# Routing attention before a tanh-shrink block: sums of the first pairs moved from TensorE products to GpSimd additions, and two masks moved behind an addition

## The chip, the cores and the metric

The kernel runs on one core of a Trainium2 chip. The metric is the time of one execution on the device in microseconds (us), the median of three runs. The engines are called as in the profile: PE (TensorE's products), PEld (its weight loads), DVE (VectorE), ACT (ScalarE), POOL (GpSimd) and SP (SyncE, which here only issues DMAs). Each engine works through its own instructions in the order in which the program gives them; engines wait for one another by semaphores.

## The reference, cut to what matters

```python
# q, k, v: (4, 8, 768, 64); centroids: (8, 16, 64)
q_assign = argmax(einsum('bhsd,hcd->bhsc', q_n, c_n))      # nearest centroid of each query
k_assign = argmax(einsum('bhsd,hcd->bhsc', k_n, c_n))      # and of each key
mask = q_assign[:, :, :, None] == k_assign[:, :, None, :]
scores = where(mask, q @ k.T / 8, -1e9)
attn = exp(scores - max(scores))
attn = attn / (sum(attn) + 1e-9)
x = (attn @ v) as (3072, 512)
h = x @ w_in                                               # 512 x 2048
out = (h - tanh(h)) @ w_out                                # 2048 x 512
```

A query attends only to keys of its own centroid. The sum over the keys divides the values' products; it is this sum whose making is changed.

## The kernel before, in words

**Pairs, halves, steps.** Two heads of a batch make a pair: 4 batches of 4 pairs, numbered n = 0 to 15 (HP = 4 pairs to a batch). The 768 queries of a pair are worked on in two halves of 384; the 768 keys are six blocks of 128, two to a step. So a half of a pair has three steps (s = 0, 1, 2), and there are 96 steps in all. Steps 0 to 11 are the first halves of pairs 0 to 3, steps 12 to 23 their second halves; then pair follows pair. Batch number 2, the third, begins at step 48 (4 * HALF, with HALF = 12).

**A step.** `begin` computes the scores of both blocks, transposed (keys on partitions), with PE (L499) into PSUM; ACT takes the exponential (L521). `select` (L531, DVE) multiplies it by a mask: is the key's code, a scalar of each partition, equal to the query's code, which lies spread over all partitions in `row`? The result is the weight `e`, 128 x 2 x 384 for a block. `value` (L556, PE) multiplies `e` with the values and accumulates over the three steps. The sum over the keys is made in one of two ways:

- `summed` pairs: `sum_up` (L571) multiplies every `e` with 32 columns of ones on PE, four products a step, accumulating in PSUM over the three steps.
- all others: GpSimd adds the six `e` of the half elementwise (L543 for the first two, L547 for each of the other four), and one pair of products with 64 columns of ones at the end, in `total` (L590), sums over the partitions.

Before, `summed` holds for the first halves of pairs 0 to 3, steps 0 to 11. In these the exponential of ACT goes to SBUF and not back to PSUM. In three of them, pairs 1 to 3 (`masked`), no mask of DVE is needed: PE adds a large negative number to the scores where codes differ, by a product of one-hot codes (`hot`, made by `one_hot`, L474 and L478 on DVE, from codes that come by a DMA; the product is L510). In pair 0 DVE masks: twelve instructions whose inputs `row` and `e` both lie in SBUF. For all later masked halves the exponential lies in PSUM, and L531 reads `row` from SBUF and `sc` from PSUM.

**What stands around it.** In the first twelve steps PE also transposes queries and keys of pairs 2 and 3 (`turn`, L355), compares them with the centroids (`similar`, L376) and transposes codes for publishing (`publish`, L432, pq); DVE makes codes of the comparison (`turn_back` L386, `route` L394 to L400, `route_on` L409), and these go through DRAM back into `hot`. `begin(following)` is called inside a step before its own `value`, so scores run one step ahead. The one_hot of pair 1 stands in DVE's order behind the masks of pair 0 and in front of the routing of pair 2. The weights of the second block arrive in pieces: `fetch` (L218) issues a DMA from GpSimd's queue, ACT prepares a piece (`rest_of`, L149 and L150), DVE finishes it (`round_piece`, L158 and L161), and then issues the next fetch on GpSimd.

**What becomes of a sum.** `total` copies it by ACT (L595). For pairs 0 and 1 it is written by DMA to DRAM, read back compactly, inverted and spread (`compact`, `invert`, `spread_out`, `scale` with L692). For pairs 2 and 3 (`soon`) it stays: `pick` (L702, PE) joins the two parts that a `summed` half leaves, `divide` (L707, L710, DVE) inverts it; GpSimd keeps tallies (L597, L711).

**Order.** The order in each step is written out by hand: a list `todo` holds small pieces of work (masks first, then transposes, publishing, routing, rounding), and a list `now` holds products of the second block (`fill`) that fit into the step. `todo` is cut into as many parts as `now` has slots, and each product calls `between()`, which does the next part. From step 24 on the products of the second block are made with seven products in place of eight (Strassen's form); product 1 of a block is copied by ACT, product 2 is added to it by DVE (L928), which frees its PSUM bank. Three banks (`ps_f`) go round. Ahead of step 48's work DVE makes the differences that the later products need (`right_factors`, L899).

Of the kernel before, what the change touches and what calls it, by code (L numbers as in the profile page):

```python
# [58 lines left out]
def kernel(  # L59
# [19 lines left out]
    HP = H // 2  # L79
# [99 lines left out]
    def fast():  # L179
# [224 lines left out]
        def route_on(n: int):  # L404
            top = tops.pop(n)
            shape = [P, 2, 2, NCH] if masked(n, 0) else [P, 2, NCH, 2]
            code = codes[n] = codep.tile(shape, F32, name="code")
            if masked(n, 0):
                nc.vector.reduce_max(  # L409
                    out=code.rearrange("p h i j -> p (i j) h"),  # L410
                    in_=top.rearrange("p (g h) c -> p g h c", h=2), axis=AX.X,
                )
                return
            nc.vector.reduce_max(out=code.rearrange("p i j h -> p (i j h)"), in_=top, axis=AX.X)

        def summed(n: int, half: int):

            return n < HP and half == 0

        def masked(n: int, half: int):  # L420


            return summed(n, half) and n > 0

        def publish(n: int):

# [56 lines left out]
        xT, scores, weights, sums, avs = {}, {}, {}, {}, {}  # L483

        def weight_tiles(n: int, half: int, s: int):
            if (n, half, s) == (0, 0, NS - 1):
                return [gp.tile([P, 2, TB], F32, name="e", tag="g") for _ in range(2)]
            t = ep.tile([P, 2, 2, TB], F32, name="e")
            return [t[:, i] for i in range(2)]

        def begin(step):
            n, half, s = step
            sc = {}
            for i in range(2):
                j = 2 * s + i
                sc[i] = ps_s.tile([P, 2, 512], F32, name="sc", tag="s")
                for h in range(2):
                    r = slice(h * D, h * D + D)
                    nc.tensor.matmul(  # L499
                        sc[i][:, h, 0:TB],  # L500
                        lhsT=turned[n, 1][r].rearrange("p a n -> p (a n)")[:, j * P : (j + 1) * P],
                        rhs=turned[n, 0][r, half], start=True, stop=not masked(n, half),
                    )
            for i in range(2):
                j = 2 * s + i
                out = sc[i][:, :, 0:TB]
                if masked(n, half):
                    for h in range(2):
                        r = slice(h * D, h * D + D)
                        nc.tensor.matmul(  # L510
                            sc[i][:, h, 0:TB],
                            lhsT=hots[n][r, 1].rearrange("p a n -> p (a n)")[:, j * P : (j + 1) * P],
                            rhs=hots[n][r, 0, half], start=False, stop=True,
                        )
                if summed(n, half):
                    if i == 0:
                        weights[n, half, s] = weight_tiles(n, half, s)
                    out = weights[n, half, s][i]
                else:
                    scores[n, half, j] = sc[i]  # L520
                nc.scalar.activation(out=out, in_=sc[i][:, :, 0:TB], func=ACT.Exp, scale=SCALE)  # L521

        def select(n: int, half: int, j: int):

            if not masked(n, half):
                if j % 2 == 0 and not summed(n, half):
                    weights[n, half, j // 2] = weight_tiles(n, half, j // 2)
                e = weights[n, half, j // 2][j % 2]
                sc = e if summed(n, half) else scores.pop((n, half, j))
                for h in range(2):  # L530
                    nc.vector.scalar_tensor_tensor(  # L531
                        out=e[:, h].rearrange("p (j n) -> p j n", n=P), in0=rows[n, half][:, h],
                        scalar=(
                            codes[n][:, h, 1, j : j + 1] if masked(n, 0) else codes[n][:, 1, j, h : h + 1]
                        ),
                        in1=sc[:, h, 0:TB].rearrange("p (j n) -> p j n", n=P),
                        op0=ALU.is_equal, op1=ALU.mult,
                    )
            if j % 2 == 1 and not summed(n, half):
                pair = weights[n, half, j // 2]  # L540
                if j == 1:
                    s = sums[n, half] = sump.tile([P, 2, TB], F32, name="sum")
                    nc.gpsimd.tensor_tensor(out=s, in0=pair[0], in1=pair[1], op=ALU.add)  # L543
                else:
                    s = sums[n, half]
                    for i in range(2):
                        nc.gpsimd.tensor_tensor(out=s, in0=s, in1=pair[i], op=ALU.add)  # L547

        def value(n: int, half: int, s: int):
            e = weights.pop((n, half, s))  # L550
            if s == 0:
                avs[n, half] = ps_a.tile([P, TB], F32, name="av", tag="a")
            for i in range(2):
                j = 2 * s + i
                for h in range(2):
                    nc.tensor.matmul(  # L556
                        avs[n, half][h * D : h * D + D], lhsT=vals[n][:, h, j], rhs=e[i][:, h],
                        start=(j == 0), stop=(j == NCH - 1),
                    )
            if summed(n, half):  # L560
                weights[n, half, s] = e

        def sum_up(n: int, half: int, s: int):
            e = weights.pop((n, half, s))
            if s == 0:
                sums[n, half] = ps_f.tile([P, TB], F32, name="den", tag="f")
            for i in range(2):
                for h in range(2):

                    r = h * D + i * D // 2  # L570
                    nc.tensor.matmul(  # L571
                        sums[n, half][r : r + D // 2], lhsT=ones[:, 0 : D // 2], rhs=e[i][:, h],
                        start=(s == 0), stop=(s == NS - 1), tile_position=(0, r),
                    )
# [311 lines left out]
        def right_factors(b: int, c: int):  # L886

            if c == 0:
                diffs[b] = (
                    late_pools["diff"].tile([P, 3, CH, TB], F32, name="diff")  # L890
                    if b else half_pools["diff"].tile([P, 3, CH, TB // 2], F32, name="diff")
                )
            d = diffs[b]
            x, y = columns(b, c), columns(b, CH + c)
            for out, u, w in (
                (d[:, 0, c], x[:, 1], x[:, 0]), (d[:, 1, c], y[:, 1], d[:, 0, c]),
                (x[:, 1], y[:, 1], x[:, 1]), (d[:, 2, c], y[:, 0], d[:, 1, c]),
            ):
                nc.vector.tensor_tensor(out=out, in0=u, in1=w, op=ALU.subtract)  # L899
# [174 lines left out]
        HALF = HP * NS  # L1074
# [122 lines left out]
        route(1)  # L1197
        route_on(1)
        begin(steps[0])
        round_piece(rounding.pop(0))  # L1200
        begin(steps[1])
        publish(1)
        select(*steps[0][:2], 0)
        spread_both(1)
        begin(steps[2])
        load(1, (2,))
        load(3)
        for n in range(2, HP):
            load(n, (2,))
        select(*steps[0][:2], 1)  # L1210
        ready[1] = {**ready.get(1, {}), 5: lambda: one_hot(1)}

# [10 lines left out]
        for at, (n, half, s) in enumerate(steps):  # L1223
# [13 lines left out]
            now = []  # L1237
# [3 lines left out]
                spent += now[-1][0]  # L1241
            stages = ready.get(at, {})

            values_first = 1 in stages and not summed(n, half)
            if values_first:
                value(n, half, s)
            if 1 in stages:
# [16 lines left out]
                    rest_of(piece)  # L1264
            if not values_first:
                value(n, half, s)
            if summed(n, half):
                if 0 in stages:
                    stages.pop(0)()
                sum_up(n, half, s)  # L1270
            if s == NS - 1:
                take(n, half)
# [30 lines left out]
            if following:  # L1303
                todo += [lambda i=i: select(*following[:2], 2 * following[2] + i) for i in range(2)]

                if half == 1 and s == NS - 1 and joined(n):
                    todo.insert(len(todo) - 1, lambda n=n: total_both(n))
# [33 lines left out]
            if "raw" in late_pools:  # L1341
                todo += [check_done, check_done, check_on, check_on]
                if p == HP - 1 and half == 1 and s == NS - 2:
                    todo += [lambda b=b, c=c: right_factors(b, c) for c in range(CH - 1)]
            slots = max(sum(it[1] for it in now), 1)
            if at == 2 * HALF:
                for c in range(CH):
                    right_factors(0, c)
# [17 lines left out]
            if at in fills and "raw" in late_pools:  # L1366
                for c in range(CH - 1 if at > 4 * HALF else 0, CH):
                    right_factors(b - 1, c)
            for it in now:
                it[2](between)  # L1370
            if not now:
                between()
        for it in late:
# [222 lines left out]
```

## Time and profile before

| | |
|---|---|
| median of 3 runs | 957.53 us (957.04 to 958.78) |
| the profiled execution | 958.52 us |
| its span, first to last instruction | 956.7 us |
| PE busy | 941.8 us (98%) |
| DVE busy | 571.2 us (60%) |
| POOL busy | 512.1 us (54%) |
| ACT busy | 292.6 us (31%) |
| L571, sums by 32 columns | 96 records of 498 ns, 10.2 us busy |
| L590, sums by 64 columns | 40 records of 486 ns, 8.2 us busy |
| L547, additions of GpSimd | 112 of 1852 ns |
| L543, the first addition of a half | 28 of 1879 ns |
| L531, masks with PSUM input | 336 of 608 ns |
| L531, masks of pair 0 | 12 of 611 ns |
| granted clock of PE | 1.0 throughout |

A product of float32 stands in the records twice (two passes): the four products of a sum are eight records. Products that use different columns of the array run beside one another, so that eight records of some 500 ns take 0.85 us from the first start to the last end; what a group costs PE is better read from the start of the next. The times of a timeline row are the start, and the length from the first start to the last end of its instructions; x8 means that eight are merged.

### The profile page before, as it was taken

Reading aid. Unit: us, or ns where it says so; the run is one execution under the profiler, and the core shown is the slowest. Engines: PE = TensorE matmul, PEld = TensorE weight load, DVE = VectorE, ACT = ScalarE, POOL = GpSimd, SP = SyncE. Lnnn points to the kernel's source line nnn. Section 1 sums busy time; section 2 is a strip of 40 time slices with the busy share of each in tenths; the row PEclk is TensorE's granted clock in tenths of the full one; section 3 lists DMA queues with packets and bytes.
Section 4 is the critical chain, followed back from the end, with each engine's and each line's share of the span. In section 5 each row is a group of like instructions: output and inputs, shape, how many; then the busy total and the mean of one; then the engine's idle time right before and its main releaser. Section 6 shows DMA issues by size and latency. Waiting matters only on the chain.

```text
span 956.7 us, 16942 instructions
## 1 busy us (share of the span) xinstructions
PE 941.8 (98%) x6584; PEld 458.6 (48%) x6584; DVE 571.2 (60%) x1098; ACT 292.6 (31%) x453; POOL 512.1 (54%) x364
## 2 busy tenths in 40 slices
PE   8999999999999999999999999999999999999997
PEld 5433443345653333444455554444455555445664
DVE  7657676976776677666845567766754346443011
ACT  5575554223332332323321212333331220222000
POOL 1026353456775464777684453867796353657500
PEclk9999999999999999999999999999999999999999
DMA  7766455992736645474574746457334223323321
GB/s 196 200 188 147 141 153 128 261 258 88 196 117 157 158 143 122 151 175 130 189 191 148 181 146 184 111 179 173 110 125 146 98 81 103 116 78 132 107 106 36
DMA packets 166764, 139.85 MB, mean 146 GB/s; under 512 B 116580, under 2 KB 145044, under 8 KB 163988
## 3 DMA queue, kind: packets, MB, share of 16 engines
q1 hardware_dynamic: 160292, 117.15, 44.4%
q0 software_dynamic: 6240, 21.50, 6.8%
q8 instruction: 54, 0.88, 0.4%
q14 instruction: 34, 0.28, 0.1%
q10 hardware_dynamic: 144, 0.03, 0.0%
HBM read 117.48 MB, written 21.17 MB: 145 GB/s over the span
## 4 chain that ended last, share of the span: by engine, by line
PE 92%; DVE 2%; DMA 1%; ACT 1%; issue 1%; SPq 0%; DVEq 0%; ACTq 0%
PE pu L933 26%; PE pd L1029 23%; PE sc L499 14%; PE av L556 13%; PE o L746 8%; PE h L730 4%; PE sim L376 1%; DMA stream<-up_factors 1%; PE den L571 1%; PE den L617 1%; DVE e L531 1%; PE den L590 1%; DVE diff L899 0%; PE pq L432 0%; DVE t L348 0%
## 5 line engine op out<-in xcount | busy, mean ns | idle before, releaser
L547 POOL TENSOR_TENSOR sum<-sum,e 128x768 f32<-128x768 f32 x112 | 207.4, 1852 | 94.4 <-DVE e L531 90.2
L531 DVE SCALAR_TENSOR_TENSOR e<-row,code,sc 128x384 f32<-128x384 bf16 x336 | 185.9, 608 | 67.3 <-ACT sc L521 59.7
L521 ACT ACTIVATE sc<-sc 128x768 f32<-128x768 f32 x168 | 125.9, 789 | 229.5 <-PE sc L499 211.8
L1029 PE MATMUL pd<-stream,G 128*64 128x256 f32 x1728 | 191.2, 379 | 0.0
L933 PE MATMUL pu<-xT,stream 128*64 128x384 f32 (+1 forms) x1024 | 159.0, 447 | 1.7 <-DMA stream<-up_factors 1.1
L1029 PEld LDWEIGHTS pd<-stream,G 128*64 128x64 f32 x1728 | 123.9, 137 | 66.9 <-issue 7.2
L499 PE MATMUL sc<-t,t 64*128 64x384 f32 x768 | 150.2, 509 | 0.4 <-ACT e L521 0.3
L556 PE MATMUL av<-e,vals 128*64 128x384 f32 x768 | 145.9, 499 | 1.3 <-DVE e L531 1.3
L1002 POOL TENSOR_TENSOR G<-G,th 128x768 f32<-128x768 f32 (+1 forms) x51 | 87.1, 1724 | 69.4 <-ACT th L1000 69.2
L933 PE MATMUL pu<-diff,stream 128*64 128x384 f32 (+1 forms) x768 | 121.1, 448 | 2.8 <-DVE G L928 1.8
L933 PEld LDWEIGHTS pu<-xT,stream 128*64 128x64 f32 x1024 | 73.1, 137 | 75.8 <-issue 61.4
L499 PEld LDWEIGHTS sc<-t,t 64*128 64x128 f32 x768 | 65.9, 186 | 73.8 <-issue 37.6
L556 PEld LDWEIGHTS av<-e,vals 128*64 128x64 f32 x768 | 46.9, 136 | 86.3 <-issue 82.0
L1000 ACT ACTIVATE th<-G 128x768 f32<-128x768 f32 (+1 forms) x51 | 40.9, 806 | 148.9 <-DVE G L928 144.2
L543 POOL TENSOR_TENSOR sum<-e 128x768 f32<-128x768 f32 x28 | 52.6, 1879 | 62.8 <-DVE e L531 42.2
L746 PE MATMUL o<-w_out,g 128*64 128x512 f32 x384 | 86.1, 593 | 0.0
L933 PEld LDWEIGHTS pu<-diff,stream 128*64 128x64 f32 x768 | 53.8, 137 | 59.3 <-issue 45.2
L928 DVE TENSOR_TENSOR G<-pu,u 128x384 f32<-128x384 f32 x72 | 39.7, 552 | 32.9 <-PE pu L933 32.9
L1040 DVE SCALAR_TENSOR_TENSOR c<-pd,du 128x256 f32<-128x256 f32 x36 | 15.2, 421 | 67.1 <-PE pd L1029 67.1
L746 PEld LDWEIGHTS o<-w_out,g 128*64 128x64 f32 x384 | 27.4, 137 | 50.1 <-issue 50.0
L1040 DVE SCALAR_TENSOR_TENSOR du<-pd,du 128x256 f32<-128x256 f32 x27 | 11.4, 420 | 60.8 <-PE pd L1029 60.8
L730 PE MATMUL h<-xT,w_in 128*64 128x384 f32 x256 | 42.8, 486 | 0.0
(137 smaller groups left out, 827.0 us busy)
## 6 DMA issues: line engine op xcount, KB each, us to landing
stream<-up_factors SPq DMA_DIRECT2D x32, 896.0 KB
stream<-down_factors SPq DMA_DIRECT2D x21, 1024.0 KB
raw<-in_moe_w_in_dram POOLq DMA_DIRECT2D x16, 512.0 KB, 5.0
raw<-in_moe_w_out_dram POOLq DMA_DIRECT2D x16, 512.0 KB, 4.7
again<-in_moe_w_in_dram SPq DMA_DIRECT2D x32, 256.0 KB
again<-in_moe_w_out_dram SPq DMA_DIRECT2D x32, 256.0 KB
vals<-in_v_dram SPq DMA_DIRECT2D x32, 192.0 KB
row<-q_codes SPq DMA_DIRECT2D x29, 192.0 KB
```

Source lines behind the costliest of these rows:

```text
L499: nc.tensor.matmul(sc[i][:, h, 0:TB], lhsT=turned[n, 1][r].rearrange("p a n -> p (a n)")[:, j * P : (j + 1) * P], rhs=turned[n, 0][r, half ...
L521: nc.scalar.activation(out=out, in_=sc[i][:, :, 0:TB], func=ACT.Exp, scale=SCALE)
L531: nc.vector.scalar_tensor_tensor(out=e[:, h].rearrange("p (j n) -> p j n", n=P), in0=rows[n, half][:, h], scalar=(codes[n][:, h, 1, j : j ...
L543: nc.gpsimd.tensor_tensor(out=s, in0=pair[0], in1=pair[1], op=ALU.add)
L547: nc.gpsimd.tensor_tensor(out=s, in0=s, in1=pair[i], op=ALU.add)
L556: nc.tensor.matmul(avs[n, half][h * D : h * D + D], lhsT=vals[n][:, h, j], rhs=e[i][:, h], start=(j == 0), stop=(j == NCH - 1),)
L730: nc.tensor.matmul(h[r], lhsT=w_in[i][:, c, o * P : (o + 1) * P][:, r], rhs=xT[c][:, half], start=(c == 0), stop=(c == CD - 1),)
L746: nc.tensor.matmul(acc[sub][r], lhsT=gs[f % HF][:, f // HF, sub * P : (sub + 1) * P][:, r], rhs=w_out[f // FQ][:, f % FQ], start=(f == seq ...
L933: nc.tensor.matmul(ps[r], lhsT=streams[base + i][:, c, k_, r], rhs=right[c], start=(c == 0), stop=(c == CH - 1),)
L1000: nc.scalar.activation(out=th, in_=t, func=ACT.Tanh)
L1002: nc.gpsimd.tensor_tensor(out=t, in0=t, in1=th, op=ALU.subtract)
L1029: nc.tensor.matmul(ps[r], lhsT=left(i)[:, r], rhs=t[:, i], start=(i == 0), stop=(i == HF - 1))
```

## The change

`summed` is split in two. A new function `direct` holds for what `summed` held for, the first halves of pairs 0 to 3, and rules where the exponential and the masks go. `summed` holds only for pair 3. So the sums of pairs 0, 1 and 2 are made by fifteen additions of GpSimd, issued by `select`, and `total` makes three pairs of L590. Pair 2 loses its `pick`. At the last step of pairs 0 to 2 the pieces `rest_of` now come ahead of ACT's copy of the values (L581), and `total` comes in `todo`. At step 48 the first product's `between` does nothing, and `todo` is cut into one part fewer, so that its first part, the first two masks of the next step, comes behind the second product's addition.

```diff
+        def direct(n: int, half: int):
+
+            return n < HP and half == 0
+
         def summed(n: int, half: int):
 
-            return n < HP and half == 0
+            return n == HP - 1 and half == 0
 
         def masked(n: int, half: int):
 
-            return summed(n, half) and n > 0
+            return direct(n, half) and n > 0
...
-                if summed(n, half):
+                if direct(n, half):
                     if i == 0:
                         weights[n, half, s] = weight_tiles(n, half, s)
                     out = weights[n, half, s][i]
...
-                if j % 2 == 0 and not summed(n, half):
+                if j % 2 == 0 and not direct(n, half):
                     weights[n, half, j // 2] = weight_tiles(n, half, j // 2)
                 e = weights[n, half, j // 2][j % 2]
-                sc = e if summed(n, half) else scores.pop((n, half, j))
+                sc = e if direct(n, half) else scores.pop((n, half, j))
...
-            values_first = 1 in stages and not summed(n, half)
+            values_first = 1 in stages and not direct(n, half)
...
-            if summed(n, half):
+            if direct(n, half):
                 if 0 in stages:
                     stages.pop(0)()
+            if summed(n, half):
                 sum_up(n, half, s)
...
-            slots = max(sum(it[1] for it in now), 1)
+            slots = max(sum(it[1] for it in now) - (at == 4 * HALF), 1)
...
-            for it in now:
-                it[2](between)
+            for i, it in enumerate(now):
+
+                it[2](between if i or at != 4 * HALF else lambda: None)
```

## The prediction

> **What bounds the kernel now.** I read the page's engine sums first: PE busy for 941.8 us of a span of 956.7, GpSimd (POOL) for 512.1. So a product taken off PE is worth its length wherever PE is not waiting for something else, and the question is what PE waits for in the 50 us that the change touches. The timeline of PE from 26 us and of DVE from 21.5 us shows that.
>
> ```profile
> start us, us, engine line op out<-in xcount [idle before <-releaser]
> 26.11 0.85 PE L571 MATMUL den<-e,ones 128*32 128x384 f32 x8
> 27.11 0.86 PE L376 MATMUL sim<-t,bd 128*32 128x192 f32 x16 [0.15 <-ACT t L362]
> 27.90 1.51 PE L556 MATMUL av<-e,vals 128*64 128x384 f32 x8
> 29.34 0.85 PE L571 MATMUL den<-e,ones 128*32 128x384 f32 x8
> 30.12 1.56 PE L499 MATMUL sc<-t,t 64*128 64x384 f32 x8
> 31.52 0.49 PE L510 MATMUL sc<-hot 64*128 64x384 bf16 x4
> 31.94 1.51 PE L556 MATMUL av<-e,vals 128*64 128x384 f32 x8
> 33.38 0.85 PE L571 MATMUL den<-e,ones 128*32 128x384 f32 x8
> 34.16 0.28 PE L432 MATMUL pq<-ident,code 128*24 128x128 f32 x1
> ```
>
> A sum (L571) stands behind the values (L556) of every step; its successor starts 0.785 us after it (30.19 - 29.41 in the chain). PE has almost no gap here. DVE, in the same stretch:
>
> ```profile
> start us, us, engine line op out<-in xcount [idle before <-releaser]
> 21.58 6.46 DVE L531 SCALAR_TENSOR_TENSOR e<-row,code,e 128x384 f32<-128x384 bf16 x12 [1.11 <-DMA row<-q_codes]
> 30.17 0.42 DVE L474 TENSOR_SCALAR hot<-hot,mine_code 128x768 bf16<-128x768 bf16 x1 [2.13 <-DMA hot<-q_codes]
> 30.51 0.32 DVE L478 TENSOR_SCALAR hot<-hot,mine_code 128x384 bf16<-128x384 bf16 x1
> 30.74 0.59 DVE L386 STREAM_TRANSPOSE sim<-sim 128x384 f32<-128x384 f32 x1
> ```
>
> The reader should see: pair 0's twelve masks run without a break to 28.04; one_hot(1) then waits 2.1 us for its transfer and ends at 30.83, only 0.7 us before PE's L510 uses it at 31.52; the routing of pair 2 behind it ends at 33.70, only half a microsecond before pq (34.16). Two short slacks, both on DVE. GpSimd does no addition here: its timeline has one small copy at 21.62, eight issues of weight loads, and its first addition at 63.36. The third view is later, where GpSimd does add; DVE first, then GpSimd:
>
> ```profile
> start us, us, engine line op out<-in xcount [idle before <-releaser]
> 348.36 0.61 DVE L531 SCALAR_TENSOR_TENSOR e<-row,code,sc 128x384 f32<-128x384 bf16 x1
> 348.89 1.41 DVE L692 TENSOR_TENSOR xT<-xT,den 128x384 f32<-128x384 f32 x1
> 350.22 2.16 DVE L692 TENSOR_TENSOR xT<-xT,t 128x384 f32<-128x384 f32 x1
> ```
> ```profile
> 349.96 2.00 POOL L547 TENSOR_TENSOR sum<-sum,e 128x768 f32<-128x768 f32 x1
> ```
>
> An add before this one ran from 348.07 to 349.88. The mask with one input in PSUM (sc) keeps its 0.61 beside it. L692, both inputs in SBUF, takes 0.55 when alone (its shortest); here the two end 0.42 and 0.41 us behind the ends of the two adds (350.30, 352.38), and the second add, issued while an L692 was running, took 2.00 instead of 1.81. They take turns, each whole.
>
> **1. Sums off PE (steps 0 to 8).** Nine groups of L571 go: 9 x 0.785 = 7.07 us. Three totals (L590, two products of 64 columns, 0.72 us by half of the values' 1.44) and three ACT copies come in for them; pair 2's pick (tally L702, 0.79) falls away. By PE alone: 7.07 + 0.79 - 3 x 0.72 = 5.7 us less. Of the list DMAs on SP, pairs 0 and 1 lose two writes and one read each: a little less queue, taken as nothing.
>
> **2. Fifteen adds on GpSimd.** 1.82 us each, 27 us on an engine that is busy for 4.2 us from 22 to 62. Their length is hidden; their inputs are not. For pairs 1 and 2 they read what ACT wrote, and DVE has little to do. For pair 0 they fall among its masks. These are written e<-row,code,e: row in SBUF and e in SBUF, unlike all later masks. No row shows such a mask beside an add. From one side: the 186 later masks beside adds cost 0.61, nothing extra. From the other: L692, which pays the rest of the running add. The Trainium skill's page "SBUF — State Buffer", section "Who interferes with whom", speaks for the latter: a DVE instruction with two SBUF inputs contends with a GpSimd instruction that reads SBUF, and whoever issues second is blocked for the whole of the other. By the row of the same line the sum of pair 0 is free and the change gains; by the rule and L692 it isn't. I take L692, as operands and not the line's name are what the two rows differ in.
>
> Then, with masks 0.54 apart: mask 4 (counted from 0) starts at 23.72, the first add (needs masks 0 to 3) is issued at 23.9, waits for mask 4 and ends about 26.0; mask 5 ends 0.42 later at 26.4; the next add (needs 4 and 5) comes behind mask 6 and ends at 28.7; mask 7 at 29.1; add to 31.35, mask 9 at 31.8; add to 34.0, mask 11 at 34.45 instead of 28.04. one_hot's first half follows at once (34.8), the fifth add takes its turn to 36.6, the second half ends at 36.85: a tensor_scalar waits too (L158 took 1.24 beside an add at 69.56, 0.41 alone). Routing of pair 2 needs 2.96 more (30.74 to 33.70): 39.8. So pq is at 39.85 instead of 34.23, +5.6; sums 0 to 2, gone from PE, lie inside this wait and give nothing. The total of pair 0 behind pq adds 0.72: **+6.35 at the scores of step 4**, while PE waits for DVE.
>
> From there: sum 3 gives nothing (the next similarity, 40.40, waits for ACT's copies, which follow the same scores). Sums 4 and 5: -1.57. From pq of pair 3 to its L510 the interval stays as it is: 49.55 to 59.12 now, with its mask ready at 58.93 after publishing, two DMAs and L474/L478; the 1.57 of sums 6 and 7 less 0.72 for a total turn into a wait for that transfer. Sum 8 and the tally: -1.57; total of pair 2 +0.72. That total also waits: four adds and two fetches of 0.53 stand in GpSimd's queue from the exponentials of step 7 on, some 8.4 us, to about 0.5 us behind the values of step 8; between 0 (fetches issued earlier) and 1.5 (DVE's rounding takes turns), I take 0.5. Sum: -1.57 - 1.57 + 0.72 + 0.5 = -1.9. **First part: 6.35 - 1.9 = +4.45.**
>
> Each fetch (L218, POOL) now stands behind adds, up to 5 us later, as do the exponentials; pieces are used 5 to 18 us after their fetch, and everything behind it is late by as much, so nothing is charged. The rounding pieces (rest, 1.4 us) now go ahead of ACT's copy of pair 0 to 2; the next values start 2 us after that copy at steps 2 and 5, about at it at step 8: 0 to 0.3, taken 0.
>
> **3. The masks behind the second product's addition (step 48).** The chain of waits there (start, length, what):
>
> ```profile
> 365.14 1.14 DVE e L531 x2
> 366.27 0.48 DVE G L928
> 366.75 0.04 issue
> 366.80 0.54 PE pu L933
> ```
>
> PE stands for 1.84 us until the addition L928 frees a bank of PSUM. With the two masks behind it the addition starts at 365.14, PE at 365.75: **-1.05**. The second pair of masks then ends near 367.8 as now; the values that need them come at 369.80 - 1.05 = 368.75. GpSimd's add starts 0.5 later, with its sum due steps later. What covers the masks here is the product and the scores of step 49 (3 us); without it they would cost the same 1.05 again. Bounds: -1.1 to 0.
>
> **Sum.** 4.45 - 1.05 = +3.4: span 956.7 to 960.1, with the 1.82 around it 961.9; the profiled execution, 958.52, is 0.99 over the median, so 960.9 for the median. Later waits (the stream of 194.6 to 202.85 among them) follow program order and move along.
>
> **Rivals.** (a) Two SBUF inputs do not make a mask wait. Then tensor_scalar still does: adds run from 23.9 to 33.3 without a gap, one_hot ends near 33.5, pq waits until 36.55, scores of step 4 at +3.05: 3.05 - 1.9 - 1.05 = +0.1, 957.6. For it: the 186 masks; against it: L692. (b) Other side, faster: no operation of DVE waits here, because GpSimd's adds fall in DVE's gaps. Then pq comes at 33.75, the scores of step 4 at +0.2, and 0.2 - 1.9 - 1.05 = -2.75: 954.8. It decides in favour of the change as soon as one_hot(1) ends before about 33.5, that is when the masks lose under 3 us of the 6.4. Against it: with 5 adds of 1.82 us starting at 23.9 there is no gap to fall into. (c) The locks are right but more comes: the total of each pair waits for a full queue of GpSimd (1 us each), DVE's rounding (L161, 0.69 alone, 2.08 beside an add at 141.41) holds up the routing of pair 3: 962.5 and over.
>
> **Chances.** My case, 959.3 to 962.5, 0.52; (a) 0.2; (b) 0.17; (c) 0.11. The range takes in (a) and most of (c): 955.7 to 963.2. About 0.2% (1.9 us) is what a measurement of this kernel can tell from no change: faster 0.17, same 0.22 (case (a) and the low edge of mine), slower 0.61.
>
> **What would show it.** Right: the twelve masks of pair 0 last about 13 us instead of 6.5, some of them near 2 us, each ending 0.4 behind an add; L510 of step 3 near 37; L571 three times only; L928 of step 48 directly behind the differences, with PE's wait there about 0.8. Wrong: masks of 0.61 throughout, or a DVE end that PE doesn't wait for; then (a) or (b). A hot of pair 3 that lands sooner would give up to 0.85 more.

## The result, and the profile after

The changed kernel takes 966.48 us (median of 6 runs, 965.51 to 967.33) against 957.9 of the kernel before (6 runs): ratio 1.009, 95% interval 1.0077 to 1.0103, 8.6 us slower. The direction was forecast; the size was put at 3.4 us, and the time lies above the top of the range (963.2). The profiled executions differ by 7.9 us (966.41 against 958.52) and their spans by 7.8 (964.5 against 956.7); the profiled execution of before was about 0.6 us over its median. The lines named here have moved down by four in the file: L535 is the mask, L478 and L482 are one_hot, L503, L514, L560 scores, one-hot products and values, L594 the total, L547 and L551 GpSimd's additions, L932 the addition of step 48.

Where the time went is read from the start of each step's scores, first L499 and L503 of the step, in the two timelines. Difference, after less before:

| scores of step | 3 | 4 | 6 | 8 | 9 | 10 | 11 | 14 | 26 | 49 | 50 to 95 |
|---|---|---|---|---|---|---|---|---|---|---|---|
| us | -0.2 | +6.9 | +6.2 | +5.4 | +4.7 | +10.5 | +9.6 | +9.0 | +8.9 | +8.9 | +7.8 |

Two jumps, of 7.1 us before step 4 and 5.8 before step 10, small gains between, and 1.04 gained at step 48. DVE's timeline after has the cause of both jumps (start, length, instruction, idle time before):

```profile
21.64 12.67 DVE L535 SCALAR_TENSOR_TENSOR e<-row,code,e 128x384 f32<-128x384 bf16 x12 [1.29 <-DMA row<-q_codes]
34.56 1.85 DVE L482 TENSOR_SCALAR hot<-hot,mine_code 128x384 bf16<-128x384 bf16 x1
...
60.91 2.05 DVE L158 TENSOR_SCALAR w_in<-raw 128x512 uint32<-128x512 uint32 x1
63.10 0.69 DVE L161 CUSTOM_DVE_ANT_0 w_in<-w_in,rest 128x1024 uint16<-128x1024 uint16 x1
63.71 2.39 DVE L478 TENSOR_SCALAR hot<-hot,mine_code 128x768 bf16<-128x768 bf16 x1
66.02 1.85 DVE L482 TENSOR_SCALAR hot<-hot,mine_code 128x384 bf16<-128x384 bf16 x1
```

The twelve masks take 12.67 us in place of 6.46, and at 63.71 the one_hot of pair 3 takes 4.2 us in place of 0.73. Before, these were its rows:

```profile
58.27 0.42 DVE L474 TENSOR_SCALAR hot<-hot,mine_code 128x768 bf16<-128x768 bf16 x1 [2.19 <-DMA hot<-q_codes]
58.61 0.32 DVE L478 TENSOR_SCALAR hot<-hot,mine_code 128x384 bf16<-128x384 bf16 x1
```

GpSimd beside DVE after the change:

```profile
24.01 2.05 POOL L547 TENSOR_TENSOR sum<-e 128x768 f32<-128x768 f32 x1 [0.73 <-DVE e L535]
...
58.42 4.26 POOL L551 TENSOR_TENSOR sum<-sum,e 128x768 f32<-128x768 f32 x2 [1.37 <-ACT e L525]
...
64.06 3.70 POOL L551 TENSOR_TENSOR sum<-sum,e 128x768 f32<-128x768 f32 x2
```

Additions and masks take turns from 24.0 on, as worked out; the two additions of 64.06 to 67.76 do the same to pair 3's one_hot, which was not worked out. PE, behind both:

```profile
36.47 0.82 PE L514 MATMUL sc<-hot 64*128 64x384 bf16 x4 [4.96 <-DVE hot L482]
37.22 2.83 PE L560 MATMUL av<-e,vals 128*64 128x384 f32 x8
...
67.93 0.76 PE L514 MATMUL sc<-hot 64*128 64x384 bf16 x4 [4.09 <-DVE hot L482]
68.61 2.83 PE L560 MATMUL av<-e,vals 128*64 128x384 f32 x8
```

Two waits of 5.0 and 4.1 us, and then something new: the eight records of values behind each wait take 2.83 us, where before they took 1.51. The rows of before at the second place:

```profile
58.98 0.50 PE L510 MATMUL sc<-hot 64*128 64x384 bf16 x4
59.41 1.51 PE L556 MATMUL av<-e,vals 128*64 128x384 f32 x8
```

 The stretches around the two waits in the changed kernel say why; the columns are the stretch and its length, then each engine's busy time, PEclk, DMA share and GB/s:

```profile
31.40:36.40 5.00, 0.11 (x2) 0.10 (x1) 5.00 (x6) 0.00 (x0) 3.83 (x2) 0.75 0.94 226
36.40:40.30 3.90, 3.83 (x14) 0.99 (x13) 2.75 (x6) 3.01 (x5) 1.64 (x1) 0.50 0.00 0
...
67.90:71.20 3.30, 3.27 (x12) 1.12 (x13) 1.87 (x5) 2.74 (x5) 0.57 (x1) 0.52 0.46 129
```

The granted clock of PE falls to half 2.4 us into the first wait, at 33.9, and comes back at 40.7; the second time it falls as the wait ends, at 68.0, and comes back at 71.4. Before, it was 1.0 throughout these steps. The chain of waits at step 48 has the masks gone from ahead of the addition:

```profile
373.54 0.34 DVE diff L903
373.89 0.12 issue
374.01 0.56 DVE G L932
```

L932 follows the differences at once; PE's wait for it is 0.8 us in place of 1.84.

### The profile page after: what moved, and what is told of

Read it like the earlier page. It is cut to its first block, busy times and chain, and to the rows that moved or that the text cites. A ratio compares the mean times of both kernels' runs of the same rounds, so it can differ in the third digit from the quotient of the medians.

```text
span 964.5 us, 16833 instructions
## 1 busy us (share of the span) xinstructions
PE 940.2 (97%) x6520; PEld 458.5 (48%) x6520; DVE 588.5 (61%) x1096; ACT 293.0 (30%) x453; POOL 541.8 (56%) x379
## 4 chain that ended last, share of the span: by engine, by line
PE 91%; DVE 4%; DMA 2%; ACT 1%; issue 1%; SPq 0%; ACTq 0%; DVEq 0%
PE pu L937 26%; PE pd L1033 23%; PE sc L503 13%; PE av L560 13%; PE o L750 8%; PE h L734 4%; DVE e L535 2%; PE sim L376 1%; PE warm L302 1%; PE den L621 1%; PE den L594 1%; DMA stream<-up_factors 1%; DMA row<-q_codes 0%; DVE diff L903 0%; DVE hot L482 0%
## 5 line engine op out<-in xcount | busy, mean ns | idle before, releaser
L551 POOL TENSOR_TENSOR sum<-sum,e 128x768 f32<-128x768 f32 x124 | 231.2, 1865 | 101.7 <-DVE e L535 92.0
L535 DVE SCALAR_TENSOR_TENSOR e<-row,code,sc 128x384 f32<-128x384 bf16 x336 | 185.7, 607 | 67.2 <-ACT sc L525 56.3
L560 PE MATMUL av<-e,vals 128*64 128x384 f32 x768 | 149.1, 506 | 1.5 <-DVE e L535 1.5
L503 PE MATMUL sc<-t,t 64*128 64x384 f32 x768 | 150.0, 509 | 0.3 <-ACT e L525 0.3
L503 PEld LDWEIGHTS sc<-t,t 64*128 64x128 f32 x768 | 65.8, 186 | 74.3 <-issue 36.7
L547 POOL TENSOR_TENSOR sum<-e 128x768 f32<-128x768 f32 x31 | 58.4, 1883 | 65.0 <-DVE e L535 42.0
L560 PEld LDWEIGHTS av<-e,vals 128*64 128x64 f32 x768 | 47.7, 137 | 88.1 <-issue 83.3
L932 DVE TENSOR_TENSOR G<-pu,u 128x384 f32<-128x384 f32 x72 | 39.6, 551 | 32.9 <-PE pu L937 32.9
```

Source lines behind the costliest of these rows:

```text
L503: nc.tensor.matmul(sc[i][:, h, 0:TB], lhsT=turned[n, 1][r].rearrange("p a n -> p (a n)")[:, j * P : (j + 1) * P], rhs=turned[n, 0][r, half ...
L535: nc.vector.scalar_tensor_tensor(out=e[:, h].rearrange("p (j n) -> p j n", n=P), in0=rows[n, half][:, h], scalar=(codes[n][:, h, 1, j : j ...
L560: nc.tensor.matmul(avs[n, half][h * D : h * D + D], lhsT=vals[n][:, h, j], rhs=e[i][:, h], start=(j == 0), stop=(j == NCH - 1),)
```

## Experiments

Differences are of medians against the kernel before, run beside each kernel; shifts of a step are read as in the table above, against the profile of before. My theory after the result: turn-taking at pair 0's masks and at pair 3's one_hot, and half a clock behind each. The rival: GpSimd's load as such, late sums and late fetches.

**Which part of the change.** Four kernels differ from the changed one in one line:

```diff
         def summed(n: int, half: int):
-            return n == HP - 1 and half == 0
+            return n < HP and half == 0         # step48_only: all sums on PE
+            return 0 < n < HP and half == 0     # pair0_only
+            return n in (0, 3) and half == 0    # pairs12_only
+            return n in (0, 2, 3) and half == 0 # pair1_only
```

> Only the second part of the change: masks behind the second product's addition at step 48; all sums of pairs 0 to 3 stay on PE. Theory (the two parts are independent, PE's wait at step 48 shrinks by two masks): 1.05 us less than the kernel before, ratio 0.9989. Rival (the parts act on each other, or the wait comes back at once elsewhere): no difference.

Measured 956.48 against 957.58: ratio 0.9992 (0.9983 to 1.0), -1.1 us. In its trace step 50 gains 1.05. The interval reaches to no change; the trace shows the gain, and so do all other kernels with this edit (1.04 to 1.06 at step 50).

> The changed kernel with only pair 0's sums on GpSimd; pairs 1 to 3 on PE. Theory (port taken in turns by pair 0's masks and the adds, then half clock after the wait): almost all of the loss up to step 4, +6.9, less 1.05 of step 48, about +5.9 us against the kernel before. Rival (GpSimd's load delays fetches and sums of all pairs alike): a third of the loss, +3 - 1 = +2.

Measured 962.9: 1.0058 (1.0045 to 1.0071), +5.3. Step 4 is 7.3 us late and nothing more is lost (of the 7.3, 1.8 are back at step 49, before step 48's edit shows). The rival's +2 is out.

> The changed kernel with pair 0's sums back on PE; pairs 1 and 2 on GpSimd. Theory: the one_hot of pair 3 still takes turns with pair 2's adds (about 3.5 us) and PE drops to half clock once; against that the products saved: +2.1 in all up to step 14, less 1.05, about +1.1 us. Rival (pair 0's masks alone are the cause, as predicted): the -1.9 of the prediction less 1.05, about -3.

Measured 960.87: 1.0041 (1.0028 to 1.0054), +3.3, more than either. Scores of step 10 jump by 5.8 us as in the changed kernel, with PE waiting 4.08 us for one_hot:

```profile
60.88 0.78 PE L514 MATMUL sc<-hot 64*128 64x384 bf16 x4 [4.08 <-DVE hot L482]
61.59 2.83 PE L560 MATMUL av<-e,vals 128*64 128x384 f32 x8
```

So pair 0 isn't the only cause. A further 1.1 us is lost at step 13, where PE waits for masks that stand behind the rounding of a piece; see the fetches below.

> The changed kernel with only pair 1's sums on GpSimd. Theory: no mask and no one_hot on PE's path meets its adds; sums 4 and 5 are saved (1.57), a total is added (0.79), sum 3 lies under ACT's copies: -0.8, less 1.05, about -1.9 us. Rival (each pair on GpSimd costs about 3 us): +2.

Measured 957.49: 1.0003 (0.999 to 1.0016): no difference in place of the -1.9 expected, though the profiled execution, one of the faster, had a span of 954.4. Its twelve executions spread from 954.9 to 960.32. Another execution of the same kernel, on another chip:

> The kernel with pair 1's sums on GpSimd once more, for one look: its timed executions lie in two groups, near 955.5 and near 960, and the profile taken belongs to the faster. Theory (in some executions a piece of the second block's weights lands late, and the masks of step 13 wait for its rounding, as seen with pairs 1 and 2): if this execution is of the slower group, its step 13 waits 1 us or more; if it is of the faster, it shows nothing new. Rival: the difference lies elsewhere in the kernel.

That execution took 957.21 (one of before beside it 958.87), between the groups. Its step 13 waits for nothing; it loses 1.1 us ahead of step 7's scores instead, and 0.5 more at pair 3's one_hot. DVE's timelines of the two executions, pair1_only first:

```profile
42.23 0.42 DVE L478 TENSOR_SCALAR hot<-hot,mine_code 128x768 bf16<-128x768 bf16 x1 [2.61 <-DMA hot<-q_codes]
42.57 0.31 DVE L482 TENSOR_SCALAR hot<-hot,mine_code 128x384 bf16<-128x384 bf16 x1
```
```profile
43.48 0.42 DVE L478 TENSOR_SCALAR hot<-hot,mine_code 128x768 bf16<-128x768 bf16 x1 [3.98 <-DMA hot<-q_codes]
43.81 1.89 DVE L482 TENSOR_SCALAR hot<-hot,mine_code 128x384 bf16<-128x384 bf16 x1
```

The transfer landed 1.25 us later in the second, the addition of 43.74 came between the two halves of one_hot, the routing behind it was late, and PE's pq waited 0.94 us. The theory of step 13 fell for this execution; what the executions near 960 do was not seen.

**Is it the meeting itself?** Two kernels keep all sums on PE and only put five operations of GpSimd beside pair 0's masks:

```diff
+            if (n, half) == (0, 0) and j % 2 == 1:
+                if j == 1:
+                    sums["spare"] = sump.tile([P, 2, TB], F32, name="sum")
+                for i in range(1 if j == 1 else 2):
+                    nc.gpsimd.tensor_tensor(out=sums["spare"], in0=e_i, in1=e_i, op=ALU.add)  # spare_adds
+                    nc.gpsimd.memset(sums["spare"], 0.0)                                      # spare_memsets
```

(`e_i` stands for `weights[n, half, j // 2][i]`.) Their result is not used.

> All sums on PE as before, with step 48's edit; five additions of GpSimd on pair 0's weights beside its masks, whose result is not used. Theory (each add holds a port that masks with two SBUF inputs need): the twelve masks again take about 12.7 us and step 4 starts some 6.5 us late; +5.5 us with step 48's -1.05. Rival (the loss comes from sums that are late, not from the adds themselves): -1.05.

Measured 961.64 against 958.25: 1.0034 (1.0023 to 1.0045), +3.4. In the profiled execution, the slowest of seven with 962.91, step 4 is 4.9 late, with a stretch of half a clock behind PE's wait. Its masks:

```profile
21.52 11.43 DVE L535 SCALAR_TENSOR_TENSOR e<-row,code,e 128x384 f32<-128x384 bf16 x12 [1.16 <-DMA row<-q_codes]
```

That it is less than expected fits two things: these additions, with one tile for both inputs, take 1.48 us and not 1.82 when undisturbed, and no total is added. No sum moved, and the loss is there: it is the meeting.

> As the run with spare additions, but the five operations of GpSimd only write (memsets of the same tile, 128x768). Theory (GpSimd's reads hold what a second SBUF input needs): masks of 0.6 us throughout, -1.05 us against the kernel before. Rival (any SBUF traffic of GpSimd holds DVE up): masks stretched as with the additions.

Measured 956.8: 0.9989 (0.9978 to 1.0), -1.45, as with step 48's edit alone. DVE and GpSimd in its timelines:

```profile
21.67 6.45 DVE L535 SCALAR_TENSOR_TENSOR e<-row,code,e 128x384 f32<-128x384 bf16 x12 [1.32 <-DMA row<-q_codes]
```
```profile
23.31 3.94 POOL L547 MEMSET sum<- 128x768 f32 x5
```

Five writes of the same tile lie wholly beside the masks, and these keep their 6.45 us. Writes of GpSimd alone do not block a mask with two inputs in SBUF; additions, which also read, do.

**Can one_hot be kept out of it?** pairs12_strided takes every second element and then the others (`rearrange("p (n two) -> p two n", two=2)` on input and output of both operations):

> Pairs 1 and 2 on GpSimd, pair 0 on PE, and one_hot reads and writes every second element, then the others, so that DVE does not run it in its fast mode. Theory (its fast mode is what takes turns with the adds): one_hot takes about 1.3 us in place of 4.2, PE's wait in step 9 falls under 2 us and its clock stays: 4 us less than with pairs 1 and 2 alone, about -2.9 against the kernel before. Rival (any DVE operation from SBUF to SBUF waits): no gain against pairs 1 and 2 alone, or a loss of 0.6.

Measured 962.3: 1.0045 (1.0033 to 1.0057), +4.0: no gain. (The profiled execution, 958.75, was the fastest of six by 2.6 us; what the others lost more is not seen.) Beside the additions:

```profile
56.98 2.25 DVE L479 TENSOR_SCALAR hot<-hot,mine_code 128x768 bf16<-128x768 bf16 x1 [0.29 <-DMA hot<-q_codes]
59.13 1.97 DVE L483 TENSOR_SCALAR hot<-hot,mine_code 128x384 bf16<-128x384 bf16 x1
```

Alone, the two took 0.67 and 0.43 in this kernel (0.42 and 0.31 unstrided). 0.67 us for 768 elements is still less than the 0.96 that a transposition of 768 takes on DVE (L348). So the fast mode that the run was to leave may have stayed, and the run does not tell whether it is what waits. That stays open.

**Is it the clock, and does a full clock help?** Products that nobody reads are put on PE in both waits, eleven in all:

```diff
+            if n in (1, 3) and half == 0 and s == 0:
+                keep_warm(6 if n == 1 else 5)        # in begin, between L503 and L514
```

> The changed kernel with products that nobody reads (13 of 128 columns by 256) put on PE before the one-hot products of steps 3 and 9, six and five of them: PE works while it waits for DVE's one_hot. Theory (the granted clock falls to half behind the two waits, and that costs 1.7 and 1.8 us): about 3 us less than the changed kernel, granted clock 1.0 throughout. Rival (the products after the waits are slow for another reason, such as SBUF contention): no gain, or a loss of a few tenths.

Measured 965.92 against 958.25: 1.0087 (1.0071 to 1.0102), against 1.009 of the changed kernel: no gain. But the trace has the clock at 1.0 and values of 1.51 us behind both waits,

```profile
36.70 1.51 PE L562 MATMUL av<-e,vals 128*64 128x384 f32 x8
...
67.24 1.51 PE L562 MATMUL av<-e,vals 128*64 128x384 f32 x8
```

and step 4 is 5.8 late instead of 6.9, step 10 7.7 instead of 10.5. The products were slow because of the clock, and 2.8 us came back. Two of them were lost again at step 13. The chain of waits there:

```profile
72.10 0.47 POOL wholes L603
...
73.05 6.85 DMA raw<-in_moe_w_in_dram
...
80.63 0.77 ACT rest L150
...
82.59 2.11 DVE e L537 x4
```

A fetch stands in GpSimd's queue behind the tally `wholes`, which waits for ACT's copy of pair 2's total; the piece lands at 79.9, its rounding is late, and the masks of step 13 stand behind that. So the tally was issued a step later, everything else as in after_warm:

```diff
         def total(n: int, half: int):
             if soon(n):
-                nc.gpsimd.tensor_tensor(out=wholes, in0=wholes, in1=t, op=ALU.add)
+                if (n, half) != (2, 0):
+                    nc.gpsimd.tensor_tensor(out=wholes, in0=wholes, in1=t, op=ALU.add)
         def divide(n: int, half: int, part: int):
+            if (n, half, part) == (2, 0, 0):
+                nc.gpsimd.tensor_tensor(out=wholes, in0=wholes, in1=t, op=ALU.add)
```

> The run with unread products in PE's two waits, and in addition GpSimd's tally of pair 2 (wholes) is issued a step later, so that it does not hold up the fetches behind it. Theory (there the gain of a full clock, 2.8 us up to step 10, was given back at step 13, where PE waits for masks behind the rounding of a piece that was fetched late): step 13's wait of 2 us goes, about 2 us less than the changed kernel. Rival (the transfer itself is slow then, whenever it is issued): step 13 still waits, as slow as the changed kernel.

Measured 963.56 against 957.06: 1.0062 (1.0049 to 1.0075), +6.5 in place of after_warm's +7.7: 1.2 us gained, and 2.1 against the changed kernel, as the theory had it. Step 13 waits for nothing more, although in this execution half a clock came back in front of step 4 (values of 2.17 us), and step 4 is 6.5 late. Late fetches are a second bound, just under the first: in the changed kernel they cost nothing, because PE comes later.

**The meeting at pair 0 taken away.** Pair 0's additions wait for one_hot of pair 1, by a small copy of GpSimd that reads it:

```diff
+        def sum_first():
+            nc.gpsimd.tensor_copy(out=gate, in_=hots[1][:, 0, 0, 0:1])
+            ... # the five additions of pair 0, no longer in select
-        ready[1] = {**ready.get(1, {}), 5: lambda: one_hot(1)}
+        ready[1] = {**ready.get(1, {}), 5: lambda: (one_hot(1), sum_first())}
```

with pair 0's total a step later; pairs01_gated has pair 2's sums on PE as well.

> The changed kernel with pair 0's five additions held back until one_hot of pair 1 is done (a small copy on GpSimd reads its result first), and pair 0's total one step later. Same sums, same engines; only the meeting of masks and additions is taken away. Theory: masks of 0.6 us, scores of step 4 about 1 us late (additions now hold the weights' buffers a little) in place of 6.9; the wait for pair 3's one_hot in step 9 stays; about 5 us less than the changed kernel, +3 against the kernel before. Rival (the lateness of sums on GpSimd costs as such): as slow as the changed kernel.

Measured 964.75: 1.0088 (1.0072 to 1.0105), +7.7. The masks take 6.45 us and step 4 comes 0.7 us earlier than before: the first jump is wholly gone.

```profile
21.55 6.45 DVE L535 SCALAR_TENSOR_TENSOR e<-row,code,e 128x384 f32<-128x384 bf16 x12 [1.20 <-DMA row<-q_codes]
```

But the additions now fill GpSimd's queue from 30.8 to 51.4; the totals of pairs 0 and 1 wait 1.8 and 2.4 us for them, and pair 3's one_hot then costs its 4.1 us of waiting and half a clock as ever (a jump of 6.4 at step 10, which is 7.7 late). Of the 7.6 us saved at step 4 against the changed kernel, 2.7 are left at step 10.

> As the run with held-back additions, but pair 2's sums on PE, so that pair 3's one_hot meets no addition either. Theory (those two meetings and the half clock behind them are the whole loss): sums 4 and 5 saved, a total paid, step 48's 1.05: about -2 us against the kernel before. Rival (something else on GpSimd's queue also costs, such as late fetches): not under the run with step 48's edit alone.

Measured 959.57: 1.0028 (1.0016 to 1.0039), +2.5, where the theory had -2. The rival's part is true here: with no meeting at pair 0 and none at pair 3 (pair 2's one_hot meets additions, but PE does not wait for it), the queue is what PE waits for,

```profile
51.27 1.43 PE L607 MATMUL den<-sum,ones 128*64 128x384 f32 x4 [2.44 <-POOL sum L554]
```

and the half clock behind that wait makes it worse (1.43 us for the total, 0.87 at a full clock). Holding the additions back made this queue; in the changed kernel no total waits for GpSimd. No version with sums on GpSimd was shown to beat the kernel before; step48_only has the best claim, with an interval that ends at 1.0.

## Why the prediction was wrong

- **The masks of pair 0**: right. Predicted 12.9 us by the rows of L692, measured 12.67; the last mask ends at 34.31 (34.45 predicted), one_hot at 36.41 (36.85), pq at 39.98 (39.85). That pq fits so well is luck in part: its code was ready at 39.30, and the values at half a clock held it up. The memsets and spare additions show the cause: the row of the same operands counted, not the row of the same line. Rivals (a) and (b) are out. The time lies where (c) had it, 962.5 and over, but mostly for reasons that (c) did not name: no total waited for GpSimd, and the rounding of pieces on DVE held pair 3 up by some tenths only (below).
- **Step 4**: +6.35 predicted, +6.92 measured. After_warm puts 1.1 us of it on the half clock, which no term of my sum had (0.9 when the 0.2 by which these two executions differ at step 3 already is taken off).
- **Sums 4 and 5, 8, the tally, the totals of pairs 1 and 2**: each 0.7 to 0.9, near what was worked out. The wait of 0.5 us for pair 2's total did not come; PE came later than GpSimd.
- **The step that failed**: "From pq of pair 3 to its L510 the interval stays as it is". It went from 9.71 us (49.27 to 58.98) to 13.3 (54.63 to 67.93). I let one_hot of pair 1 take turns with an addition and forgot that pair 3's meets two: 4.24 us in place of 0.73, 3.5 us. Its start was nearly right: one_hot starts 9.1 us behind pq, 9.0 before. But what it waited for last was no longer the transfer, whose last packet landed at 63.31: DVE came to one_hot at 63.71, from a piece's rounding that an addition had stretched (L158 at 60.91, 2.05 us for 0.42). That is 0.3 us of rival (c). Pairs12_only has this jump without pair 0, pair1_only has not.
- **The term that was missing**: PE's clock. 1.1 us in front of step 4 and 1.6 in front of step 10, by after_warm against the changed kernel. I had priced the waits by their length alone, and before no wait in the middle of the kernel had cost the clock anything (the 1.84 us at step 48 are the longest).
- **Fetches**: "nothing is charged" held for the changed kernel and hid a bound two microseconds further down, which took back most of what after_warm had won.
- **Step 48**: -1.05 predicted, -1.04 measured, in every kernel that has the edit, and nothing of it given back.

The sum with the two corrected terms: 3.4 + 3.5 + 2.7 = 9.6, less the 0.5 of the wait that didn't come and 0.4 that the first products of the second block (step 14) gained: 8.7. At step 4 my sum was too long by 0.5, once the clock is taken out of the measured shift (6.9 - 1.1 = 5.8 against 6.35): 8.2, against 7.8 in the traces. The 0.4 left was not taken apart; some 0.1 to 0.2 of it is there at steps 0 to 3, ahead of anything that the change touches.

## What to carry to other kernels

Before moving work to an idle engine, list every instruction that its operands will meet, one by one along the path: here the cost was not the additions' length but seven places on the path where DVE had to wait for one to end. A wait of PE is dearer than its length when the clock follows it; after a repair look for what is late next (a fetch in the same queue, a total) before counting the gain. And when a piece of the path depends on whether a transfer lands just ahead of or behind another engine's operation, executions of the same kernel can differ, as the two of pair 1 did.

## What the runs showed of the hardware

- PE's granted clock fell to 0.5 at waits of 4.96 us (for 6.8 us, 4.3 of them behind the wait's end) and of 4.09 us (for 3.4, all of it behind the end). The Trainium skill's page "TensorE: Matmul & The Clock Gate" (section "Why this matters for your kernels") advises against idle gaps of more than about 3 us between bursts of products. Every wait of 4.08 us or more here was followed by half a clock. Shorter waits did it too, though not each time: 1.81 us in spare_adds and 2.44 in pairs01_gated were followed by 3.4 us of half clock, while 2.42 in after_gated and 2.19 in after_warm were not, and 2.19 in after_warm_wholes was. Every such stretch lasted 3.4 or 6.8 us. What decides on a short wait, no run here shows.
- GpSimd's additions slow down as well, but less: 1.82 us alone, 2.02 to 2.05 when a mask was running at their issue.
- DVE's instructions with one input in PSUM kept their times beside additions (L531 0.61 with and without), and pair 0's masks, with two inputs in SBUF, kept theirs beside GpSimd's memsets.
